# How finely the next tile's projections are dealt out over the first sixteen segments of a recurrent attention block

## The chip, the cores and the metric

The kernel runs on one core of a Trainium2 chip. The metric is the device time of one launch in microseconds (us). The matmul engine is called PE (its weight loads are shown apart, as PEld), the vector engine DVE, the scalar engine ACT, GpSimd POOL; the queue from which most DMAs are issued is that of SP.

## The reference, cut to what matters

Two mixers alternate, A, B, A, B, each with a layer norm before it and a residual behind it. A is the recurrent one, and the change is in it:

```python
for s in range(64):                       # segments of 32 rows, one after the other
    h = concat([mem, xs[s]])              # 8 memory rows + 32 rows of the sequence
    q, k, v = h @ Wq, h @ Wk, h @ Wv      # 32 heads of 128
    p = softmax(mask(q @ k.T * scale))
    o = (p @ v) @ Wo
    mem = o[:8]                           # the next segment starts from these rows
    outs.append(o[8:])
```

B is a gated MLP that mixes over the sequence; the change does not touch it. All is bf16 with float32 sums; the sequence has 2048 rows.

## The kernel before, in words

`a_block` runs twice (below: the first and the second block), each time over 64 segments. Four segments make a tile of 128 rows, so a block has 16 tiles; `tb` is the tile and `j4` the segment in it, 0 to 3.

A segment needs the last memory rows of the segment before it, so the segments are a chain. The last 8 rows of the 32 of each segment of the sequence are kept apart ("old" rows): their projections do not depend on the memory and are made ahead, for all four segments of the next tile at once. That is `b_units` (L753). It makes six chunks, named by `j`: 0 and 1 are the two halves of the queries, 2 and 3 of the keys, 4 and 5 of the values. A chunk is 16 matmuls of 512 columns (four steps of the contraction, `kt`, times four column groups that run side by side). It is summed in one bank of PSUM, either that of the pool `accA` or that of `accB`. Both pools have one buffer. In every segment `accB` serves, one after the other, the query half 1 (`psm`), the value half 1 (`psV`), the output products `px` and the chunk of old rows.

The order of PE, DVE and ACT is the order in which the program is written (`manual_schedule`). POOL and SP are ordered by the scheduler. `b_units` is a generator; `segment` (L908) calls it through `fill()`, three times a segment, at places where PE would else wait:

- fill 1, ahead of `pv(0)`: after the scores and their sums, while ACT and DVE still make the second half of the weights `E` (L960, L963);
- fill 2, after `pv(1)`: while the memory rows are normalised (`memory_out`, L1021) that `wo_pairs` (L794) needs;
- fill 3, after the output products `px` (`wo_pairs`, L794) and `pw` (`wo_rest`, L801): while DVE folds `px` (`fold`, L891 and L893), adds it to `pw` (L898) and turns the sum into the next segment's input `hT` (L900). The next segment begins with the matmuls `psQ` on that input.

Two chunks are spent per segment, one in each pool. Of the `accA` chunk four matmuls go to fill 1, eight to fill 2 and four to fill 3; the whole `accB` chunk goes to fill 3, behind them. So fill 3 has 20 matmuls. In the first 16 segments of a block a tile's six chunks are done in segments 0, 1 and 2 (order 4, 5, 0, 2, 1, 3), and segment 3 has none. From tile 4 on, segment 3 carries parts of the output product of the old rows (`y_part`). In tile 0 of the first block the next tile's chunks are made before, in segment 0.

What a chunk leaves behind is copied out of PSUM by ACT when `run(copies)` comes: after the memory rows (ahead of `wo_pairs`), and after fill 3. Value chunks go to `VB`; when both are there, `store_v` (L737) writes them to DRAM in one DMA of 256 KB, and `spread_v` (L740), called from `tail` in segment 1, reads them back in four DMAs of 64 KB as `VX`. Query and key chunks go to `rowsB` (two slots), and one DMA transpose each (L780, issued from SP) writes them to `QTB` and `KTB`.

`prep_segment` (L877) picks a segment's part from `QTB` and `KTB` on POOL: one copy to `QQ` and two to `KX` (L885), for the two halves `r` of the heads. `scores(0)` needs half 0 of `KX`, `scores(1)` half 1. In the kernel before both halves lie in one tile `KX`, of which there are two for even and odd segments. POOL also copies `hB` (L637), the old rows of the next tile's input, once per tile; it waits for the DMA transpose of `hT` (L208).

Of the kernel before, what the change touches and what calls it, by code (L numbers as in the profile page):

```python
# [7 lines left out]
BF16 = mybir.dt.bfloat16  # L8
F32 = mybir.dt.float32
# [5 lines left out]
P = 128  # L15
DM = 512
KT = 4
# [564 lines left out]
def qk_rhs(w, j, kt, cg):  # L582
    return w[j // 2][:, kt, :].rearrange("p (r gs i eb el) -> p r eb i gs el", r=2, gs=4, i=4, eb=4)[:, j % 2, cg]


def cols_rhs(w, j, kt, cg):
    at = 2048 * (j % 2) + 512 * cg
    return w[j // 2][:, kt, at:at + 512]
# [81 lines left out]
def a_block(tc, c, rows, front, MV_in, RS_in, MV_out, RS_out, ahead, wo, S, first):  # L670
    nc = tc.nc
    NSEG = S // SEG
    NB = S // P
# [3 lines left out]
    with ExitStack() as ctx:  # L677
# [12 lines left out]
        pers = ctx.enter_context(tc.tile_pool(name="a_pers", bufs=1))  # L690
# [7 lines left out]
        accA = _Tagged(acc_pool, "accA", 1)  # L698
        accB = _Tagged(acc_pool, "accB", 1)
# [7 lines left out]
        w = ahead.wqkv  # L707
# [4 lines left out]
        def mm_chunk(ps, lhs, rhs, kts=range(KT)):  # L712

            return [nc.tensor.matmul(ps[32 * cg:32 * cg + 32, :], lhsT=lhs(kt, cg), rhs=rhs(kt, cg), start=(kt == 0), stop=(kt == KT - 1),  # L714
                                     tile_position=(0, 32 * cg)) for kt in kts for cg in range(4)]
# [8 lines left out]
        NKQ = 2  # L724
        KAr = [pers.tile([P, 2, 8, 32, 2], BF16, name=f"KA{i}") for i in range(2)]
        QQr = [pers.tile([P, 2, 8, 40, 2], BF16, name=f"QQ{i}") for i in range(NKQ)]
        KXr = [pers.tile([P, 4, 2, 32], BF16, name=f"KX{i}") for i in range(NKQ)]
        uT = [pers.tile([P, H, 32], BF16, name=f"uT{i}") for i in range(2)]
        for t in uT:
            (nc.vector if first else nc.gpsimd).memset(t[:], 0.0)  # L730
# [1 line left out]
        blk_state = {}  # L732
# [4 lines left out]
        def store_v(bs):  # L737
            nc.sync.dma_start(rows.vb_d[:], bs["VB"].rearrange("p i r e -> p (i r e)"))
# [7 lines left out]
        rowsB = rowp.tile([P, 2, 512], BF16, name="rowsB", bufs=1)  # L746
        copies, turns, adds = [], [], []

        def run(todo):
            while todo:  # L750
                todo.pop(0)()

        def b_units(tb, early=0, alone=False):  # L753
            bs = blk_state[tb]
            order = (0, 2, 1, 3, 4, 5) if early else (4, 5, 0, 2, 1, 3)

            for k, j in enumerate(order):
                now = k < early
                ps = (accB if k % 2 and not alone and not (now and j == 5) else accA).tile([P, 512], F32, name="psb")[:]
                for kts in (((0,), (1, 2), (3,)), ((0, 1, 2, 3),))[k % 2 or alone]:  # L760
                    mm_chunk(ps, lambda kt, cg: bs["hB"][:, kt, :],
                             lambda kt, cg: qk_rhs(w, j, kt, cg) if j < 4 and now else cols_rhs(w, j, kt, cg), kts)
                    if kts[-1] != KT - 1:
                        yield

                def out(k=k, j=j, ps=ps, now=now):
                    if j >= 4:
                        nc.scalar.copy(bs["VB"][:, :, j - 4, :], ps.rearrange("p (i e) -> p i e", i=4))
                        if now:
                            ahead.regroup(bs["VB"], bs["VX"], (j - 4,))  # L770
                        elif j == (5 if alone else 4):
                            store_v(bs)
                        return
                    r = rowsB[:, k % 2, :]
                    nc.scalar.copy(r, ps)
                    t = bs[("QTB", "KTB")[j // 2]][:, j % 2]
                    if now:
                        turns.append(lambda: nc.vector.transpose(out=t.rearrange("p a b -> p (a b)"), in_=r))
                    else:
                        nc.sync.dma_start_transpose(out=t.rearrange("p (i g) k -> p i (g k)", g=4), in_=r.rearrange("t (i e) -> t i e", i=4))  # L780

                if now or k % 2 == 0:
                    copies.append(out)
                else:
                    copies.insert(0, out)
                if now or k % 2 or alone:
                    yield

        def wo_pairs(px, lhs):
# [81 lines left out]
        def y_norm(tb, store):  # L871
            rows.y_norm(tb, MV_out[:, tb, 0:1], RS_out[:, tb:tb + 1], store)
# [4 lines left out]
        def prep_segment(s, eng=nc.gpsimd):  # L877
            tb, j4 = s // 4, s % 4
            bs = blk_state[tb]
            QQ = QQr[s % NKQ]  # L880
            eng.tensor_copy(QQ[:].rearrange("p r n q two -> p (r n) two q")[:, :, :, 32:40],
                            bs["QTB"].rearrange("p r (n two) k -> p (r n) two k", two=2)[:, :, :, 8 * j4:8 * j4 + 8])
            KX = KXr[s % NKQ]
            for r in range(2):
                eng.tensor_copy(KX[:, :, r].rearrange("p g (k i) -> p i g k", i=4),  # L885
                                      bs["KTB"][:, r].rearrange("p (i g) k -> p i g k", i=4)[:, :, :, 8 * j4:8 * j4 + 8])
            seg_state[s] = dict(QQ=QQ, KX=KX, VX=bs["VX"])

# [19 lines left out]
        def segment(s, fill, spare1, spare2, spare3, tail, loads):  # L908
            tb, j4 = s // 4, s % 4
            st = seg_state.pop(s)  # L910
            QQ, KX, VX = st["QQ"], st["KX"], st["VX"]
# [10 lines left out]
            def qk(j, ps, copy=nc.scalar.copy):  # L922
                mms = mm_chunk(ps, lambda kt, cg: hA_cur[:, kt, :], lambda kt, cg: qk_rhs(w, j, kt, cg))
                r = rowp.tile([P, 512], BF16, name="rows", tag="rowsQK", bufs=3)
                return r, mms, copy(r[:].rearrange("p (n el two) -> p n el two", n=8, two=2), ps.rearrange("p (n two el) -> p n el two", n=8, two=2))  # L925
# [7 lines left out]
            def ends(q):  # L933

                return q.rearrange("p h (b e) -> p h b e", e=8)[:, :, 0:5:4, :]

            def own(q):

                return q.rearrange("p (i b e) -> p i b e", i=4, b=2)
# [4 lines left out]
            def scores(r):  # L944

                pS = psS[:, r, :]
                mms = []
                for i in range(4):
                    for g in range(4):
                        n = 4 * i + g  # L950
                        mms.append(nc.tensor.matmul(pS[32 * g:32 * g + 32, 40 * i:40 * i + 40], lhsT=KA[:, r, n // 2, :, n % 2], rhs=QQ[:, r, n // 2, :, n % 2],  # L951
                                                    start=(i == 0), stop=True, tile_position=(0, 32 * g), skip_group_check=True))
                for g in range(4):
                    q = QQ[:, r].rearrange("p (i g) q two -> p i g two q", i=4)[:, :, g // 2, g % 2, :]
                    mms.append(nc.tensor.matmul(own(pS[32 * g:32 * g + 32, 160:224]), lhsT=KX[:, g, r, :], rhs=ends(q),  # L955
                                                start=False, stop=True, tile_position=(0, 32 * g), skip_group_check=True))
                return mms

# [73 lines left out]
            r2, mms, _ = qk(2, psQ[:, 1, :])  # L1032
# [86 lines left out]
            if s + 1 < NSEG:  # L1119
                prep_segment(s + 1)  # L1120
# [28 lines left out]
        def values(units):  # L1149
            for n in (3, 1):  # L1150
                for _ in range(n):
                    next(units)
                run(copies)
                yield

        for s in range(NSEG):
            tb, j4 = s // 4, s % 4
            if first and s == 0:
                more = values(units)
            elif j4 > 0 and tb == NB - 1:  # L1160
                more = y_part(tb // 4, j4 - 1, last=True)
            elif j4 == (3 if tb < NB - 1 else 0) and tb > 3:
                more = y_part(tb // 4 - 1, tb % 4)
            elif first and s == 1:
                more = iter(())
            elif j4 == (first and tb == 0):
                more = b_units(tb + 1)
            if j4 == (tb == 0) and tb + 2 < NB:
                rows.load(tb + 2, first, nc.sync)

# [47 lines left out]
                        y_stats(NB - 6, k)  # L1218

            def tail():  # L1220
                if j4 == 1 + 2 * (first and tb == 0) and tb + 1 < NB:
                    spread_v(blk_state[tb + 1])
                if tb == NB - 1:
                    if j4 != 2:
                        front.load_w(j4)
                    if j4 > 0:
                        front.load_rows(j4 - 1)
                if ys and ys[0][1]:
                    y_norm(ys.pop(0)[0], nc.sync)
                for y in ys:  # L1230
                    y[1] = True
                if j4 == 0 and tb > 7 and (tb % 4 == 0 or tb == NB - 1):
                    due.extend(range(tb // 4 * 4 - 8, tb // 4 * 4 - 4) if tb < NB - 1 else range(NB - 8, NB - 4))
# [20 lines left out]
        ends = (uT[NSEG % 2], oBs[NB // 4 - 1][:, :, 96:128])  # L1254
# [52 lines left out]
```

## Time and profile before

| what | us |
|---|---|
| three runs | 1625.49, 1628.31, 1628.37 (median 1628.31) |
| the profiled execution's own time | 1627.99 |
| its span, first to last instruction | 1626.3 |
| granted PE clock, mean | 0.999 |
| PE busy | 1579.0 (97%) |
| ACT, DVE, POOL busy | 1047.4, 1065.8, 290.4 |

A line of the profile's timeline gives start, duration, engine, line, operation, output and inputs, and the number of instructions merged into it; in brackets the idle time of the engine just before it and what ended that. A matmul's record covers its whole way through the engine, so records of matmuls that follow each other overlap. Below, a segment's length is taken from one start of the exponential of `scores(0)` (the first L960 of a segment) to the next. In the second block these starts are at 919.58, 929.61, 939.65, 949.68 and 959.32 us for the four segments of tile 2 and the first one of tile 3.

### The profile page before, as it was taken

Reading aid. Unit: us, or ns where it says so; the run is one execution under the profiler, and the core shown is the slowest. Engines: PE = TensorE matmul, PEld = TensorE weight load, DVE = VectorE, ACT = ScalarE, POOL = GpSimd, SP = SyncE. Lnnn points to the kernel's source line nnn. Section 1 sums busy time; section 2 is a strip of 40 time slices with the busy share of each in tenths; the row PEclk is TensorE's granted clock in tenths of the full one; section 3 lists DMA queues with packets and bytes.
Section 4 is the critical chain, followed back from the end, with each engine's and each line's share of the span. In section 5 each row is a group of like instructions: output and inputs, shape, how many; then the busy total and the mean of one; then the engine's idle time right before and its main releaser. Section 6 shows DMA issues by size and latency. Waiting matters only on the chain.

```text
span 1626.3 us, 90252 instructions
## 1 busy us (share of the span) xinstructions
PE 1579.0 (97%) x40647; PEld 976.1 (60%) x40670; DVE 1065.8 (66%) x3052; ACT 1047.4 (64%) x2281; POOL 290.4 (18%) x604
## 2 busy tenths in 40 slices
PE   5899999999999999999999999999999999999999
PEld 2556566666666666566656555666666666665565
DVE  4566666667776776784466666666677667767722
ACT  3677777777777777660047777777777777766400
POOL 6111111112211221320011111111121112224000
PEclk9999999999999999999999999999999999999999
DMA  9412111123321343377951222122232223425797
GB/s 362 96 41 47 43 43 43 43 43 82 84 46 43 87 85 77 92 183 162 213 156 46 46 46 46 47 46 47 72 92 71 47 71 96 97 53 171 140 191 169
DMA packets 263611, 148.97 MB, mean 92 GB/s; under 512 B 197561, under 2 KB 239649, under 8 KB 263225
## 3 DMA queue, kind: packets, MB, share of 16 engines
q1 hardware_dynamic: 249992, 99.38, 28.2%
q0 software_dynamic: 13232, 43.82, 8.3%
q8 instruction: 318, 5.21, 1.3%
q14 instruction: 69, 0.56, 0.1%
HBM read 59.68 MB, written 37.19 MB: 60 GB/s over the span
## 4 chain that ended last, share of the span: by engine, by line
PE 53%; DVE 2%; DMA 1%; issue 1%; POOL 1%; ACT 0%; POOLq 0%; SPq 0%
PE pg L397 9%; PE psQ L714 7%; PE psK L714 7%; PE psb L714 5%; PE px L794 4%; PE psm L714 3%; PE psV L714 3%; PE psO L801 3%; PE pz L296 3%; PE py L440 2%; PE pwB L813 1%; PE psO L1000 1%; PE psT L992 1%; PE psS L951 1%; PE psS L974 0%
## 5 line engine op out<-in xcount | busy, mean ns | idle before, releaser
L714 PEld LDWEIGHTS <-hT 128*32 128x32 bf16 x12288 | 338.5, 97 | 274.1 <-DVE hT L900 13.3
L928 DVE STREAM_TRANSPOSE QQ<-rows 128x256 f32<-128x256 f32 x256 | 113.3, 443 | 80.9 <-ACT rows L925 79.8
L714 PE MATMUL psV<-Wv_sb,hT 128*32 128x512 bf16 x2048 | 165.6, 379 | 0.0
L1024 DVE TENSOR_TENSOR uT<-psO,Rt 128x384 bf16<-128x384 f32 x256 | 140.2, 548 | 29.2 <-ACT Rt L1100 28.8
L925 ACT CAST rows<-psQ 128x512 bf16<-128x512 f32 x256 | 142.8, 594 | 23.3 <-PE psQ L714 22.7
L960 ACT ACTIVATE S<-psS 128x224 bf16<-128x224 f32 x256 | 92.2, 360 | 97.5 <-PE psS L955 97.3
L1021 DVE TENSOR_TENSOR uT<-psO,Rm 128x128 bf16<-128x128 f32 x256 | 74.6, 291 | 122.6 <-ACT Rm L1018 120.6
L397 PE MATMUL pg<-z,wspT 128*128 128x344 bf16 x1024 | 154.3, 309 | 0.0
L714 PE MATMUL psK<-Wv_sb,hT 128*32 128x512 bf16 x2048 | 152.7, 378 | 0.0
L1100 ACT ACTIVATE Rt<-Rt 128x512 f32<-128x512 f32 x256 | 147.2, 622 | 4.1
L928 DVE STREAM_TRANSPOSE KA<-rows 128x256 f32<-128x256 f32 x256 | 112.9, 441 | 53.5 <-ACT rows L925 46.5
L714 PE MATMUL psQ<-Wq_sb,hT 128*32 128x512 bf16 x2048 | 135.8, 381 | 11.6 <-DVE hT L900 6.8
L794 PEld LDWEIGHTS <-uT 128*32 128x32 bf16 x4608 | 122.4, 97 | 34.4 <-DVE uT L1021 3.6
L794 PE MATMUL px<-Wo,uT 128*32 128x256 bf16 x3840 | 133.7, 273 | 2.1 <-issue 0.8
L714 PE MATMUL psQ<-Wk_sb,hT 128*32 128x512 bf16 x2048 | 135.5, 381 | 0.0
L714 PE MATMUL psK<-Wk_sb,hT 128*32 128x512 bf16 x2048 | 134.8, 379 | 0.0
L714 PE MATMUL psm<-Wq_sb,hT 128*32 128x512 bf16 x2048 | 134.8, 379 | 0.0
L885 POOL COPY KX<-old 128x128 bf16<-128x128 bf16 x128 | 68.3, 534 | 364.0 <-PE psS L955 225.7
L1097 ACT ACTIVATE Rt<-psT 128x1024 f32<-128x1024 f32 x128 | 131.1, 1024 | 3.1
L397 PEld LDWEIGHTS <-wspT 128*128 128x128 bf16 x1024 | 100.2, 98 | 53.2
L801 PE MATMUL psO<-Wo_high,uT 128*32 128x128 bf16 x7168 | 125.8, 219 | 4.1 <-issue 3.5
L885 POOL COPY KX<-front 128x128 bf16<-128x128 bf16 x126 | 65.2, 524 | 347.5 <-PE psS L955 202.0
(200 smaller groups left out, 2913.8 us busy)
## 6 DMA issues: line engine op xcount, KB each, us to landing
o_d<-o_sb SPq DMA_DIRECT2D x126, 64.0 KB
vb_d<-front SPq DMA_DIRECT2D x30, 256.0 KB
VX<-vb_d SPq DMA_DIRECT2D x120, 64.0 KB
ln_x<-xd SPq DMA_DIRECT2D x26, 256.0 KB
y_o<-o_d POOLq DMA_DIRECT2D x22, 256.0 KB, 3.2
xd<-y_o POOLq DMA_DIRECT2D x22, 256.0 KB, 3.0
Wq_sb<-in_A_Wq_dram POOLq DMA_DIRECT2D x8, 512.0 KB, 9.3
Wk_sb<-in_A_Wk_dram POOLq DMA_DIRECT2D x8, 512.0 KB, 10.0
```

The lines of the kernel that those rows point to most:

```text
L397: nc.tensor.matmul(pg[t][:, k, 0:344], lhsT=wsp[t][:, st, :], rhs=z(st, 344 * k, 344 * k + 344), start=(st == 0), stop=(st == NT - 1))
L714: return [nc.tensor.matmul(ps[32 * cg:32 * cg + 32, :], lhsT=lhs(kt, cg), rhs=rhs(kt, cg), start=(kt == 0), stop=(kt == KT - 1), tile_posi ...
L794: nc.tensor.matmul(px[at:at + 32, 0:256], lhsT=lhs[:, h, :], rhs=wo_rhs(h, slice(k + 2, None, -2) if h % 2 else slice(k, None, 2)), start= ...
L801: nc.tensor.matmul(pw[32 * cg:32 * cg + 32, :], lhsT=lhs[:, h, :], rhs=wo_rhs(h, cg), start=False, stop=(h == H - 1), tile_position=(0, 32 ...
L885: eng.tensor_copy(KX[:, :, r].rearrange("p g (k i) -> p i g k", i=4), bs["KTB"][:, r].rearrange("p (i g) k -> p i g k", i=4)[:, :, :, 8 * ...
L925: return r, mms, copy(r[:].rearrange("p (n el two) -> p n el two", n=8, two=2), ps.rearrange("p (n two el) -> p n el two", n=8, two=2))
L928: nc.vector.transpose(out=(QQ[:, j % 2, :, 0:32] if j < 2 else KA[:, j % 2]).bitcast(F32).rearrange("p n q one -> p n (q one)"), in_=r[:]. ...
L960: return nc.scalar.activation(out=S[:, r], in_=psS[:, r, 0:224], func=ACT.Exp, scale=scale)
L1021: nc.vector.tensor_tensor(out=hview(uT_cur[:], r, 24, 32), in0=oview(r, 0, 8), in1=Rm[:, r].rearrange("p g (n q) -> p g n q", q=8), op=ALU ...
L1024: nc.vector.tensor_tensor(out=hview(uT_nxt[:], r, 0, 24), in0=oview(r, 8, 32), in1=rview(r, 0, 24), op=ALU.mult)
L1097: nc.scalar.activation(out=Rt[:], in_=psT[:], func=ACT.Ln)
L1100: nc.scalar.activation(out=rt, in_=rt, func=ACT.Exp, scale=-1.0)
```

## The change

For tiles 0 to 3 of a block (where the next tile's chunks are not made otherwise) `b_even` takes the place of `b_units`. It spends one and a half chunks in each of the four segments: nothing in fill 1, eight matmuls of an `accA` chunk in fill 2, and one whole `accB` chunk (16 matmuls) in fill 3. Chunk 4 is spread over segments 0 and 1 beside 5 and 0; chunk 2 over segments 2 and 3 beside 1 and 3. The copies of chunks 4 and 2 thus fall ahead of `wo_pairs` in segments 1 and 3, those of the others behind fill 3. `store_v` moves from the end of segment 0 to the middle of segment 1, `spread_v` from segment 1 to segment 2. The last key chunk, 3, is finished at the very end of segment 3. In all segments of both blocks `KX` becomes two tiles, one for each half `r`.

This concerns tiles 1, 2, 3 of the first block and 0, 1, 2, 3 of the second: seven tiles, 28 segments.

```diff
-        KXr = [pers.tile([P, 4, 2, 32], BF16, name=f"KX{i}") for i in range(NKQ)]
+        KXr = [[pers.tile([P, 4, 32], BF16, name=f"KX{i}{r}") for r in range(2)] for i in range(NKQ)]
...
+        def b_out(bs, slot, j, ps, turned, stored):
...
+        def b_mms(bs, j, ps, kts, turned=False):
+            mm_chunk(ps, lambda kt, cg: bs["hB"][:, kt, :],
+                     lambda kt, cg: qk_rhs(w, j, kt, cg) if j < 4 and turned else cols_rhs(w, j, kt, cg), kts)
...
+        def b_even(tb):
+
+            bs = blk_state[tb]
+            for j, others in ((4, (5, 0)), (2, (1, 3))):
+                psA = accA.tile([P, 512], F32, name="psb")[:]
+                for kts, other in zip(((0, 1), (2, 3)), others):
+                    yield
+                    b_mms(bs, j, psA, kts)
+                    if kts[-1] == KT - 1:
+                        copies.append(lambda j=j, psA=psA: b_out(bs, 0, j, psA, False, True))
+                    yield
+                    psB = accB.tile([P, 512], F32, name="psb")[:]
+                    b_mms(bs, other, psB, range(KT))
+                    copies.append(lambda other=other, psB=psB: b_out(bs, 1, other, psB, False, False))
+                    yield
...
-                eng.tensor_copy(KX[:, :, r].rearrange("p g (k i) -> p i g k", i=4),
+                eng.tensor_copy(KX[r][:].rearrange("p g (k i) -> p i g k", i=4),
...
-                    mms.append(nc.tensor.matmul(own(pS[32 * g:32 * g + 32, 160:224]), lhsT=KX[:, g, r, :], rhs=ends(q),
+                    mms.append(nc.tensor.matmul(own(pS[32 * g:32 * g + 32, 160:224]), lhsT=KX[r][:, g, :], rhs=ends(q),
...
-                more = b_units(tb + 1)
+                more = (b_even if tb < 4 else b_units)(tb + 1)
...
-                if j4 == 1 + 2 * (first and tb == 0) and tb + 1 < NB:
+                if j4 == (3 if first and tb == 0 else 2 if tb < 4 else 1) and tb + 1 < NB:
                     spread_v(blk_state[tb + 1])
```

`b_out` holds, word for word, what the function `out` inside `b_units` did. The order of POOL changes where one tile goes over into the next: before, the three copies of one segment stand together; after, POOL's order there is `QQ`, `QQ`, `hB`, `KX` half 0 of segment 0, half 0 of segment 1, half 1 of segment 0, half 1 of segment 1. On SP the transposes stand one by one instead of in pairs, and in segment 3 the order is the transpose of `hT` (L208), the load of the rows (L196), the transpose of chunk 2, the store of the output (L906), the transpose of chunk 3.

More of the change, by code (lines that the diff above doesn't have):

```diff
@@ L751, in run @@
                 todo.pop(0)()
+        def b_out(bs, slot, j, ps, turned, stored):
+            if j >= 4:
+                nc.scalar.copy(bs["VB"][:, :, j - 4, :], ps.rearrange("p (i e) -> p i e", i=4))
+                if turned:
+                    ahead.regroup(bs["VB"], bs["VX"], (j - 4,))
+                elif stored:
+                    store_v(bs)
+                return
+            r = rowsB[:, slot, :]
+            nc.scalar.copy(r, ps)
+            t = bs[("QTB", "KTB")[j // 2]][:, j % 2]
+            if turned:
+                turns.append(lambda: nc.vector.transpose(out=t.rearrange("p a b -> p (a b)"), in_=r))
+            else:
+                nc.sync.dma_start_transpose(out=t.rearrange("p (i g) k -> p i (g k)", g=4), in_=r.rearrange("t (i e) -> t i e", i=4))
+        def b_mms(bs, j, ps, kts, turned=False):
+            mm_chunk(ps, lambda kt, cg: bs["hB"][:, kt, :],
+                     lambda kt, cg: qk_rhs(w, j, kt, cg) if j < 4 and turned else cols_rhs(w, j, kt, cg), kts)
         def b_units(tb, early=0, alone=False):
@@ L760, in b_units @@
                 for kts in (((0,), (1, 2), (3,)), ((0, 1, 2, 3),))[k % 2 or alone]:
-                    mm_chunk(ps, lambda kt, cg: bs["hB"][:, kt, :],
-                             lambda kt, cg: qk_rhs(w, j, kt, cg) if j < 4 and now else cols_rhs(w, j, kt, cg), kts)
+                    b_mms(bs, j, ps, kts, now)
                     if kts[-1] != KT - 1:
@@ L766, in out @@
                 def out(k=k, j=j, ps=ps, now=now):
[L767 to L780, printed above, removed]
+                    b_out(bs, k % 2, j, ps, now, j == (5 if alone else 4))
                 if now or k % 2 == 0:
```

## The prediction

> **What bounds the kernel now.** First the page: how busy each engine is.
>
> ```profile
> span 1626.3 us, 90252 instructions
> PE 1579.0 (97%) x40647; PEld 976.1 (60%) x40670; DVE 1065.8 (66%) x3052; ACT 1047.4 (64%) x2281; POOL 290.4 (18%) x604
> ```
>
> PE is the bound by a wide margin, so what the change is worth lies in PE's idle time inside the 28 segments it touches. Next, the sums by stretch for the four segments of tile 2 in the second block and the first of tile 3 (columns: stretch and length, then busy time of each engine).
>
> ```profile
> 919.58:929.61 10.03, 10.03 (x312) 6.16 (x304) 6.46 (x19) 7.69 (x18) 1.50 (x4) 1.00 0.12 37
> 929.61:939.65 10.04, 10.04 (x312) 6.15 (x304) 6.46 (x19) 7.70 (x19) 1.51 (x4) 1.00 0.23 55
> 939.65:949.67 10.02, 10.02 (x312) 6.16 (x304) 6.46 (x19) 7.68 (x18) 0.67 (x2) 1.00 0.17 36
> 949.67:959.32 9.65, 8.75 (x280) 5.28 (x272) 6.96 (x20) 6.93 (x16) 2.33 (x6) 1.00 0.37 59
> ```
>
> A segment with two chunks (32 matmuls) takes 10.03 us and PE shows no hole; the one with none takes 9.65 with 0.90 of hole. The first three differ from the last by 32 matmuls but by 0.38 us only. If a matmul cost just its issue time, sharing out evenly would gain. So the third view is where the holes of the empty segment lie (the timeline, its three waits):
>
> ```profile
> 951.18 0.39 DVE L963 TENSOR_TENSOR E<-S,maskN 128x448 bf16<-128x448 bf16 x1
> 951.63 0.45 PE L992 MATMUL psT<-E,ones 64*128 64x512 bf16 x4
> ...
> 953.74 0.26 ACT L1095 COPY cross<-px 64x128 f32<-64x128 f32 x1 [0.72 <-PE px L794]
> ...
> 955.15 0.61 PE L714 MATMUL psQ<-Wq_sb,hT 128*32 128x512 bf16 x8 [0.68 <-DVE hT L900]
> ```
>
> and the fourth is the end of a full segment, around fill 3:
>
> ```profile
> 923.82 0.28 DVE L891 COPY cross<-px 64x128 f32<-64x128 f32 x1 [0.60 <-PE px L794]
> 924.21 0.29 DVE L893 TENSOR_TENSOR t<-px,cross 128x128 f32<-128x128 f32 x1
> 924.37 1.25 PE L714 MATMUL psb<-Wv_sb,hB 128*32 128x512 bf16 x20
> 924.60 0.29 DVE L898 TENSOR_TENSOR memT<-psO,t 128x128 bf16<-128x128 f32 x1
> 924.99 0.37 DVE L900 STREAM_TRANSPOSE hT<-memT 128x64 bf16<-128x64 bf16 x2
> 925.45 0.60 PE L714 MATMUL psQ<-Wq_sb,hT 128*32 128x512 bf16 x8
> ```
>
> The 20 matmuls start in five rounds of four, at 924.37 and 925.45 for the next work: (925.45 - 924.37) / 5 = 0.216 us a round. `accB` is still held by `px` until L893 has read it, at 924.21 + 0.29 = 924.50. PE starts 0.06 after a DVE result (951.18 + 0.39 = 951.57, `psT` at 951.63), so a matmul into `accB` can start at 924.56. Today the first round goes to `accA` and the second, into `accB`, starts at 924.59: the wait is there, just hidden.
>
> **The change part by part.**
>
> *Fill 1 loses four matmuls: 0.* `psT` starts 0.06 after `E` in both kinds of segment: 951.63 - 949.68 = 1.95 us into the empty one, and 921.53 - 919.58 = 1.95 into a full one. The hole takes the round for nothing, so taking it out gives nothing back.
>
> *Fill 2 keeps its eight: 0.* In segment 3 they are new, and with fill 3 they make it a segment like the others.
>
> *Fill 3 goes from 20 to 16: -0.03.* Its first round now goes to `accB`, so it starts at 924.56, not 924.37, and its four rounds end at 924.56 + 4 x 0.216 = 925.42, against 925.45. The input `hT` is no limit there: in the empty segment `psQ` follows the start of L900 (954.85) by 0.30, which puts it at 925.29 in the full one. So a segment with 1.5 chunks takes 10.00 us. Bounds: 9.87 if the `px` wait were nothing (fill 3 would end at 925.23, and `hT` at 925.29 decide), 10.03 if nothing is gained.
>
> *Segment 3: +0.35* (9.65 to 10.00).
>
> Sum of a tile of the second block: -3 x 0.03 + 0.35 = +0.26, for four tiles +1.04.
>
> *First block.* Its segments measure 10.03, 10.03, 10.11 and 9.66. At the end of segment 1 two small ACT operations of the row statistics stand in the list of copies ahead of the chunk. Before, the `accB` copy was put in front of them; now it is appended behind, so `psm`, which needs `accB`, comes later. Ln and Exp take 0.30 + 0.20, about 0.45 in line; the copy ends 7.64 us into the segment, and `psm` would start 5.84 + 1.73 = 7.57: late by 0.13 with the 0.06. Tile: 4 x 10.00 + 0.13 - 39.83 = +0.30, for three tiles +0.9.
>
> *Moved at no cost.* The copies of chunks 4 and 2 by ACT (0.56 each) fall ahead of `cross`, where ACT has the 0.72 of idle time shown; if that were gone, `cross` and with it L893 would be late by the rest. The one copy less behind fill 3 lets the `rows` casts begin earlier, but PE is not waiting for them: from `psQ` to the scores takes 4.17 in both kinds of segment. `store_v` and the four `spread_v` DMAs come a segment later and have one segment left; SP's waits for them hold back only output stores and transposes that nobody needs within 5 us. The split of `KX` changes no instruction.
>
> *The tile's seam: +2.1.* Chunk 3 now ends with segment 3, and `scores(1)` of the very next segment needs what comes of it: ACT copy, SP issue, DMA transpose, POOL copy of `KX` half 1. Before, the same chain had a whole empty segment. Its rows (SP, then POOL; normal, then late; last the `hB` copy that POOL now has ahead of `KX`):
>
> ```profile
> 946.90 2.50 SPq L780 DMA_TRANSPOSE old<-rowsB  x2
> 949.46 0.48 POOL L885 COPY KX<-old 128x128 bf16<-128x128 bf16 x1 [9.35 <-DMA old<-rowsB]
> 986.64 3.56 SPq L780 DMA_TRANSPOSE front<-rowsB  x2
> 990.85 0.46 POOL L885 COPY KX<-front 128x128 bf16<-128x128 bf16 x1 [11.01 <-PE psS L974]
> 957.26 0.29 POOL L637 COPY hB<-hT 128x128 bf16<-128x128 bf16 x1 [3.23 <-DMA hT<-ln_xn]
> ```
>
> The issue comes 946.90 - 939.65 = 7.25 us into the segment, `scores(1)` loads `KX` at 5.84 + 4.97 = 10.81. Less 0.48 for the copy and 0.06, issue to copy may take 3.02. It takes 2.56 normally and 4.21 in the late row; at 27 tile ends that I can pair, eight lie above 3.02, late by 0.19 to 1.20, in the mean over all 0.19. New beside it: the transpose of chunk 2 stands on SP behind that of `hT` and the row load (1.19 + 0.57, up to 1.87 for the load alone), and POOL's `KX` half 0 stands behind it and behind `hB`, which lands up to 2.3 us into the segment; `scores(0)` needs it at 3.76. I add 0.11, an estimate from these rows. 7 x 0.30 = 2.1; ends 0 and 7 x 1.20 = 8.4.
>
> Here a rule speaks against the change. A `KX` copy takes 0.48 alone and up to 0.70 beside DVE's work. The Trainium skill, SBUF — State Buffer, "Who interferes with whom", says that a DVE instruction with two SBUF inputs and a GpSimd instruction that reads SBUF exclude each other. By it a late `KX` copy would also wait for the first `E` (0.35): 7 x 8/27 x 0.35 = 0.7 more, 1632.7 in place of my time. The trace agrees as far as it goes: the copy of 0.70 at 952.65 lies beside a DVE operation of 952.34 that took 0.68, where the same one took 0.54 at 912.52.
>
> Sum: 1.04 + 0.9 + 2.1 = +4.0, against the profiled execution's own 1627.99: **1632.0 us**. That execution lies 0.3 below the median 1628.31. About 0.2% (3.3 us) is what a measurement of this kernel can tell from no change; slower begins at 1631.6.
>
> **Rivals.** *The seam is in time.* The mean chain has 0.46 to spare (3.02 - 2.56). For it: 19 of 27 rows. Against: seven tiles, each with three transposes and a load near the seam. 1627.99 + 1.9 = 1629.9, no measurable change. *The seam is always late*, the three transposes queueing up: 7 x 1.0 (the mean of the upper four late rows) = 7.0, 1627.99 + 1.9 + 7.0 = 1636.9. *The `px` wait is no wait* (not slower): if L893 came 0.19 us earlier against PE, fill 3 would start at 924.37 and the segment take 9.87. A second-block tile would be 39.48 for 39.74, a first-block one 39.61 for 39.83: 4 x -0.26 + 3 x -0.22 = -1.7, with the seam in time 1626.3. It decides from an L893 that ends at 924.31; all full segments show it at 924.50 against the same PE rows, so I give it little. Only with scatter on top would it count as faster. *The change does nothing* to the order is out: the built program has it, with the wait on DVE ahead of fill 3's first matmul.
>
> **How the numbers follow.** Forecast (seam late now and then) 0.58; in time 0.24; always late 0.12; fill 3 without its wait 0.06. Of the forecast's cases about 7 in 10 lie above 1631.6. Slower 0.58 x 0.7 + 0.12 + 0.02 of the second = 0.55; same 0.39; faster 0.06, from the last case and unseen ones. Range 1628.5 to 1637.0: the second case less 1.4 of scatter (the three runs spread 2.9), the third with a little over.
>
> **What would show it.** Right: segments of 10.00 in all four places, 0.2 of PE idle time ahead of fill 3 released by L893, `psT` still 1.95 in. At the seam some waits of PE for POOL's `KX`, up to a microsecond, and none elsewhere. Wrong: segments at 9.7 to 9.85, or seams with no wait at all, or with one in each tile.

## The result, and the profile after

The changed kernel took 1634.62 us (median of six runs, 1633.75 to 1638.72); the kernel before took 1628.34 beside it (six runs, 1625.49 to 1629.61). The ratio is 1.0048, with a 95% interval of 1.0033 to 1.0062. A ratio here is worked out from all runs and not from the two medians: by it the change is about 7.8 us slower, by the medians 6.3. The profiled execution's own time was 1633.75 us.

The page first, as for the kernel before:

```profile
span 1632.0 us, 90242 instructions
PE 1589.4 (97%) x40670; PEld 982.4 (60%) x40670; DVE 1067.9 (65%) x3052; ACT 1049.9 (64%) x2281; POOL 288.6 (18%) x604
```

PE's share stands at 97% as before, in a kernel that is slower with the same matmuls. The share says nothing about this change.

Now the sums by stretch, each from one start of the exponential of `scores(0)` to the next. The first stretch is segment 3 of tile 1 of the second block, then come the four segments of tile 2 and the first two of tile 3 (columns: stretch and length, then busy time and instructions of PE, PEld, DVE, ACT, POOL, then granted clock, DMA share and GB/s).

```profile
914.42:924.42 10.00, 9.93 (x304) 6.34 (x296) 6.92 (x20) 7.82 (x19) 1.82 (x5) 1.00 0.36 76
924.42:934.84 10.42, 10.13 (x304) 6.39 (x296) 6.47 (x19) 7.35 (x18) 2.05 (x6) 1.00 0.05 12
934.84:944.83 9.99, 9.92 (x304) 6.35 (x296) 6.46 (x19) 7.83 (x18) 1.49 (x3) 1.00 0.18 54
944.83:954.83 10.00, 9.94 (x304) 6.37 (x296) 6.47 (x19) 7.32 (x18) 0.20 (x1) 1.00 0.19 45
954.83:964.82 9.99, 9.93 (x304) 6.33 (x296) 6.92 (x20) 7.80 (x18) 1.83 (x5) 1.00 0.39 77
964.82:976.58 11.76, 10.13 (x304) 6.40 (x296) 6.58 (x19) 7.36 (x18) 1.98 (x6) 1.00 0.03 9
976.58:986.58 10.00, 9.93 (x304) 6.42 (x296) 6.47 (x19) 7.84 (x19) 1.49 (x3) 1.00 0.22 63
```

All stretches hold the same 304 matmuls. Five of the seven take 10.00, whichever place they have in the tile. The two that don't, 10.42 and 11.76, are the first segments of a tile.

The end of an undisturbed segment (that of 934.84), from the timeline:

```profile
939.07 0.28 DVE L914 COPY cross<-px 64x128 f32<-64x128 f32 x1 [0.59 <-PE px L817]
939.46 0.29 DVE L916 TENSOR_TENSOR t<-px,cross 128x128 f32<-128x128 f32 x1
939.80 1.05 PE L714 MATMUL psb<-Wq_sb,hB 128*32 128x512 bf16 x16
939.85 0.29 DVE L921 TENSOR_TENSOR memT<-psO,t 128x128 bf16<-128x128 f32 x1
940.18 0.37 DVE L923 STREAM_TRANSPOSE hT<-memT 128x64 bf16<-128x64 bf16 x2
940.66 0.61 PE L714 MATMUL psQ<-Wq_sb,hT 128*32 128x512 bf16 x7
```

(From here on the changed file's lines are meant: those behind the new functions lie 23 further down, so `t` of L893 is L916 and the `KX` copy of L885 is L908.) The fold ends at 939.46 + 0.29 = 939.75; fill 3 starts 0.05 later and `psQ` 0.86 after that. Fill 3 now has 16 matmuls, waits for `px` in the open, and the segment ends 0.03 earlier than the full one of before. The wait hardly shows as idle time of PE, since the record of the last matmul of `pw` reaches to 939.80. It shows in the starts: that matmul starts at 939.58, so the first of fill 3 comes 0.22 behind it, where in the kernel before it came 0.05 behind (924.33 and 924.37).

The long segment of 964.82 begins with the seam from tile 2 to tile 3. SP's queue, then POOL, then PE's weight loads, in three answers of the timeline:

```profile
958.09 1.19 SPq L208 DMA_TRANSPOSE hT<-ln_xn  x1
959.33 0.57 SPq L196 DMA_DIRECT2D ln_x<-xd  x1
960.00 1.97 SPq L768 DMA_TRANSPOSE old<-rowsB  x1
962.07 0.55 SPq L929 DMA_DIRECT2D o_d<-o_sb  x1
962.73 1.20 SPq L768 DMA_TRANSPOSE old<-rowsB  x1
```

```profile
963.77 0.77 POOL L908 COPY KX<-old 128x128 bf16<-128x128 bf16 x2 [2.91 <-DMA old<-rowsB]
966.88 1.06 POOL L908 COPY KX<-old 128x128 bf16<-128x128 bf16 x3 [2.34 <-DMA old<-rowsB]
```

```profile
967.40 0.10 PEld L978 LDWEIGHTS <-KX 128*32 128x32 bf16 x4 [1.70 <-POOL KX L908]
```

SP works from 958.09 to 963.93 with gaps of no more than 0.11. The transpose of chunk 3 is the fifth in line and is issued 962.73 - 954.83 = 7.90 us into segment 3; its data lets POOL begin half 1 of `KX` only at 966.88, and PE loads it at 967.40, 12.57 into the stretch that began at 954.83. An undisturbed seam loads it at 10.80. That is 1.77 us in one place.

Who waits for `KX`, over the whole span (the view of one tile; after each name: microseconds, times), first in the kernel after, then in that before:

```profile
who waited for it (us, times):
  POOL KX L908: 367.3, 70
...
  PEld L978: 5.0, 8
  PE psS L978: 4.1, 7
```

```profile
who waited for it (us, times):
  POOL KX L885: 427.8, 81
  ACT S L960: 97.3, 127
  POOL QQ L881: 43.7, 62
  POOL front L174: 0.6, 2
```

PE's weight loads wait for `KX` eight times in the kernel after, and never before. (The row counts idle time alone; where a load is late, the loads behind it shift too.) Taken against the normal places of the two loads (9.59 us into segment 3 for half 0, half 1 1.21 later; in the last seam 0.26 is left out, by which its segment 3 is longer without a wait for `KX`), the seven seams lose 0.87, 0.36, 0.14 (first block) and 1.05, 0.44, 1.77, 1.14 (second): 5.8 us. Half 0 has 1.55 of it, in three seams; half 1 has 4.2.

The account: the seven tiles and the tile behind each block's last seam take 7.1 us longer than before (2.05 in the first block, 5.02 in the second). The forecast's terms for the segments, 1.94, and the 5.8 of the seams make 7.7; a segment of 10.68 in the second block that is 10.35 now gives back 0.3 of that. That is 7.4, or 0.3 more than measured. The two spans differ by 5.7 only, for stretches that the change does not touch moved as well: +0.6 us ahead of these tiles, +1.5 between the two blocks, -3.4 behind the last of them. So the loss is read from the tiles, and not from the spans.

### The profile page after: what moved, and what is told of

Read it like the earlier page. It is cut to its first block, busy times and chain, and to the rows that moved or that the text cites. A ratio compares the mean times of both kernels' runs of the same rounds, so it can differ in the third digit from the quotient of the medians.

```text
span 1632.0 us, 90242 instructions
## 1 busy us (share of the span) xinstructions
PE 1589.4 (97%) x40670; PEld 982.4 (60%) x40670; DVE 1067.9 (65%) x3052; ACT 1049.9 (64%) x2281; POOL 288.6 (18%) x604
## 3 DMA queue, kind: packets, MB, share of 16 engines
q8 instruction: 318, 5.21, 1.3%
## 4 chain that ended last, share of the span: by engine, by line
PE 53%; DVE 1%; DMA 1%; ACT 1%; issue 1%; POOL 0%; DVEq 0%; POOLq 0%; SPq 0%
PE pg L397 9%; PE psQ L714 6%; PE psK L714 6%; PE psb L714 5%; PE pz L296 5%; PE px L817 4%; PE psm L714 3%; PE psV L714 3%; PE psO L824 3%; PE py L440 2%; PE pwB L836 2%; PE psO L1023 1%; PE psT L1015 1%; PE psS L974 1%; PE pw L1282 0%
## 5 line engine op out<-in xcount | busy, mean ns | idle before, releaser
L817 PEld LDWEIGHTS <-uT 128*32 128x32 bf16 x4608 | 123.2, 97 | 32.4 <-issue 2.3
L908 POOL COPY KX<-old 128x128 bf16<-128x128 bf16 x128 | 65.9, 531 | 311.0 <-PE psS L978 191.0
L824 PEld LDWEIGHTS <-uT 128*32 128x32 bf16 x7168 | 114.2, 97 | 2.7 <-issue 1.5
```

The costliest lines, as they stand in the source:

```text
L817: nc.tensor.matmul(px[at:at + 32, 0:256], lhsT=lhs[:, h, :], rhs=wo_rhs(h, slice(k + 2, None, -2) if h % 2 else slice(k, None, 2)), start= ...
L824: nc.tensor.matmul(pw[32 * cg:32 * cg + 32, :], lhsT=lhs[:, h, :], rhs=wo_rhs(h, cg), start=False, stop=(h == H - 1), tile_position=(0, 32 ...
```

## The experiments

The theory: with its segments at 10.00 the change costs 1.9, and the rest is the seam, where the keys come too late by way of SP's queue. The rivals: the rest is something else that the change moved (the split of `KX`, the values' store, ACT's copies); PE is bound by its matmuls, and an even share would gain if the rounds were placed rightly; the 1634.62 was chance. Ratios are to the kernel before, whose median was 1626.0 in the one set of runs (the keys by DVE, the keys first, the split, the rounds 1, 1, 4) and 1625.9 in the other.

### The changed kernel again

> The kernel after once more, on the chip of this call, as a measure for the run with the rows loaded by ACT. Theory: ratio 1.004 to 1.005, segments of 10.00, five to seven of fourteen seam places late, 4 to 6 us of waits. Rival (the first profile of the kernel after caught an unusual execution): waits of 2 us or less, as forecast.

1632.41 us, ratio 1.0043 (1.0031 to 1.0056). Another profile of the same program lost 1.06, 0.76 and 0 at the seams of the first block, where the first one lost 0.87, 0.36 and 0.14, and 1.26, 0.55, 0.17 and 0.95 at those of the second; the sum is 4.75 us. The account closes here too: 1.94 and 4.75 less 0.3 are 6.4, and the same tiles take 6.6 longer than in the kernel before. Its rows of who waited for `KX`:

```profile
  PEld L978: 3.9, 7
  PE psS L978: 3.0, 5
```

The waits at the seam are there again, in other sizes from seam to seam. The change is slower by 0.4 to 0.5%, and not by chance.

### The keys turned by DVE in place of the DMA

```diff
 def b_even(tb):
+    def out(slot, j, ps):
+        if j not in (2, 3):
+            return b_out(bs, slot, j, ps, False, j == 4)
+        r = rowsB[:, slot, :]
+        nc.scalar.copy(r, ps)
+        t = bs["KTB"][:, j % 2]
+        adds.append(lambda: nc.vector.transpose(out=t.rearrange("p a b -> p (a b)"), in_=r))
+    def mms(j, ps, kts):
+        b_mms(bs, j, ps, kts, j in (2, 3))
...
-                    b_mms(bs, j, psA, kts)
+                    mms(j, psA, kts)
...
```

> The kernel after, but the two key chunks of b_even are turned by DVE at the end of their segment instead of by a DMA transpose, so KX does not wait for SP at the tile's seam. Theory (segments of 10.00 us each, +1.9 us in all, and the rest of the loss is the late KX at seven seams): segments of 10.00, no wait for KX, 1630.2 us, ratio 1.0012. Rival (the loss lies in the evenly spent segments themselves, the seam is only where it shows): ratio stays at 1.004 to 1.005. Second rival (only the seam costs): ratio 1.000 or below.

1628.95 us, ratio 1.0015 (1.0006 to 1.0024), or by the ratio 2.4 us over the kernel before. Segments take 9.99 to 10.00, the first one behind a seam 10.08 (the turn on DVE costs it 0.08), and PE waits for no `KX`. So without the chain over SP and POOL at the seam about 2 us are left, which is what the segments cost; two thirds of the loss are the seam.

### The keys first

```diff
-            for j, others in ((4, (5, 0)), (2, (1, 3))):
+            for j, others in ((2, (3, 0)), (4, (1, 5))):
...
-                        copies.append(lambda j=j, psA=psA: b_out(bs, 0, j, psA, False, True))
+                        copies.append(lambda j=j, psA=psA: b_out(bs, 0, j, psA, False, False))
...
-                    copies.append(lambda other=other, psB=psB: b_out(bs, 1, other, psB, False, False))
+                    copies.append(lambda other=other, psB=psB: b_out(bs, 1, other, psB, False, other == 5))
```

The same work in the same share, every DMA transpose kept, but the keys are done in segments 0 and 1 and the values last; the values come too late for their tile, which uses older ones.

> The kernel after with the chunks in the order 2, 3, 0, 4, 1, 5, so keys and queries are ready a segment before the seam; all DMA transposes stay. The value chunks come too late for their round trip through DRAM, so the old rows' values of the tile before are used: the output is not the reference's. Theory: no wait for KX at the seam, segments of 10.00, ratio 1.0012 like the turn by DVE. Rival (it is the single DMA transposes spread over the tile, not their lateness): ratio stays at 1.004 or above.

1626.37 us, ratio 1.0003 (0.9991 to 1.0014). The last two segments of tile 2 of the second block and the first of tile 3:

```profile
942.03:952.03 10.00, 9.93 (x304) 6.36 (x296) 6.46 (x19) 7.32 (x18) 1.17 (x3) 1.00 0.11 23
952.03:962.02 9.99, 9.92 (x304) 6.35 (x296) 6.92 (x20) 7.80 (x18) 1.95 (x5) 1.00 0.25 77
962.02:972.02 10.00, 10.00 (x304) 6.46 (x296) 6.58 (x19) 7.32 (x18) 1.51 (x4) 1.00 0.22 51
```

No seam waits for `KX`, and the seam's part of the loss is gone. So it is not the transposes as such, but that the last of them starts at the very end of the tile. The expected 1.9 us lie inside the interval; this run alone would also allow 0.

### The row load issued by ACT

```diff
-                rows.load(tb + 2, first, nc.sync)
+                rows.load(tb + 2, first, nc.scalar if tb < 5 else nc.sync)
```

> The kernel after with the load of the rows (L196) issued by ACT a segment later, in tiles 0 to 4, so SP has one DMA less between the transpose of hT and those of chunks 2 and 3. Theory (the seam is late because SP still works off that queue when the copy of chunk 3 is ready, 7.25 us into segment 3): the transpose of chunk 3 is issued 0.4 to 0.6 us earlier, the waits for KX fall from 6 us over seven seams to about 2, ratio 1.002 to 1.003. Rival (the transposes land late whatever SP does): the waits stay, ratio 1.005.

1629.86 us, ratio 1.0025 (1.0013 to 1.0036). SP's queue at the seam from tile 2 to tile 3 of the second block (segment 3 begins at 954.23):

```profile
957.49 1.19 SPq L208 DMA_TRANSPOSE hT<-ln_xn  x1
958.77 2.00 SPq L768 DMA_TRANSPOSE old<-rowsB  x1
960.86 0.51 SPq L929 DMA_DIRECT2D o_d<-o_sb  x1
961.49 1.19 SPq L768 DMA_TRANSPOSE old<-rowsB  x1
```

(The load stays in segment 3; ACT issues it 6.1 us into the segment, where SP did at 4.5.) One DMA of some 0.6 us less on SP ahead of the transpose of chunk 3, and that is issued 7.26 us into the segment, though chunk 2's transpose again took 2.00. Over the seven seams the issue comes at 7.31 in the mean, against 7.87 in both profiles of the changed kernel, and 1.55 us of waits remain of 5.8 and 4.75:

```profile
  PEld L978: 1.3, 3
  PE psS L978: 1.0, 3
```

In this set of runs the changed kernel stood at 1.0043, so the move saves some 2.9 us, about what the waits lost. SP's queue is the larger part of the seam's loss, with one limit: the load's own traffic moved by 1.6 us too, and no run parts the two.

### The split of KX alone

```diff
-        KXr = [pers.tile([P, 4, 2, 32], BF16, name=f"KX{i}") for i in range(NKQ)]
+        KXr = [[pers.tile([P, 4, 32], BF16, name=f"KX{i}{r}") for r in range(2)] for i in range(NKQ)]
```

with the two places that use it, and nothing else of the change.

> The kernel before with only KX split into two tiles, one for each half. Theory: no segment changes, ratio 1.000 within 0.001. Rival (the split tiles or POOL's other order cost time in all 128 segments): a part of the 1.005.

1626.94 us, ratio 1.0004 (0.9995 to 1.0013), segments of 10.03 and 9.65 as before. No gain or cost is seen; the interval alone would allow up to 2 us.

### The kernel before without fill 1

```diff
                 for kts in (((0,), (1, 2), (3,)), ((0, 1, 2, 3),))[k % 2 or alone]:
-                    mm_chunk(...)
+                    short = not (k % 2 or alone or now)
+                    if not short or kts != (0,):
+                        mm_chunk(..., kts, int(short))
```

The first quarter of the contraction is left out in the chunks that go to `accA`, in all tiles but those made ahead. These are the chunks 4, 0 and 1, and not 4, 0 and 2 as the expectation has it. The profile counts 40670 weight loads of PE in the kernel before and 40322 here, so 348 matmuls are gone (the expectation has 360): 87 rounds of 0.216, or 18.8 us by PE's issue time.

> The kernel before with fill 1 left out in every tile: the first quarter of the contraction of the chunks 4, 0 and 2 is not computed (360 matmuls, 90 rounds of 0.216 us, 19.4 us of PE time less), so the output is not the reference's. Theory (fill 1 lies in a hole until E is there): segments stay at 10.03, ratio 1.000. Rival (PE is the bound by its count): segments of 9.81, 19 us less, ratio 0.988.

1627.04 us, ratio 1.0007 (0.9995 to 1.0019). The first segment of tile 2 of the second block:

```profile
918.34:928.37 10.03, 10.03 (x308) 6.21 (x300) 6.47 (x19) 7.70 (x19) 1.49 (x4) 1.00 0.11 37
```

308 matmuls take the same 10.03 as 312 did. A round in fill 1 is free; to take it away, as the change does, gives nothing back.

### Rounds 0, 1, 5: fill 3 begins with the other bank

```diff
+                    mms(j, psA, kts[:1])
                     yield
-                    b_mms(bs, j, psA, kts)
+                    mms(j, psA, kts[1:])
+                    if kts[-1] == KT - 1:
+                        copies.append(lambda j=j, psA=psA: out(0, j, psA))
                     psB = accB.tile([P, 512], F32, name="psb")[:]
...
+                    copies.insert(0, lambda other=other, psB=psB: out(1, other, psB))
```

Keys turned by DVE as above, and one of the two `accA` rounds of fill 2 put at the front of fill 3 (20 matmuls again). All copies now fall behind fill 3, and that of `accB` goes to the front of their list, as in the kernel before.

> Keys turned by DVE, rounds 0, 1, 5: four matmuls into accA stand ahead of the accB chunk in fill 3, instead of in fill 1. Theory (an accA round in fill 3 costs nothing because accB is not free before L893 has read px): measured from the 9.80 of rounds 1, 1, 4 the wait of 0.18 is filled by a round of 0.216, so segments of 9.83 to 9.84, ratio 0.997. Rival (there is no such wait, a round more in fill 3 costs its 0.216): segments of 10.02, ratio 1.001.

1624.16 us, ratio 0.9990 (0.9979 to 1.0000). The first two segments of tile 2 of the second block, and the end of the second one:

```profile
919.88:929.71 9.83, 9.83 (x304) 6.07 (x296) 6.47 (x19) 7.31 (x18) 1.56 (x4) 1.00 0.04 12
929.71:939.54 9.83, 9.76 (x304) 5.91 (x296) 6.47 (x19) 7.70 (x18) 1.55 (x3) 1.00 0.12 23
```

```profile
934.13 0.29 DVE L929 TENSOR_TENSOR t<-px,cross 128x128 f32<-128x128 f32 x1
934.30 0.39 PE L714 MATMUL psb<-Wv_sb,hB 128*32 128x512 bf16 x4
934.52 1.03 PE L714 MATMUL psb<-Wq_sb,hB 128*32 128x512 bf16 x16
```

The fold (L929 here) ends at 934.42. The round into `accA` starts at 934.30, before that, and the first into `accB` at 934.52 with no hole between. The same 24 matmuls take 9.83 for 10.00. That gain of 0.17 is two things at once: a round less in fill 2, and a round more in fill 3. The next section parts them: the rounds 1, 1, 4 also leave one round in fill 2, have four in fill 3 and take 9.80. Against them the fifth round of fill 3, 0.216 long, makes the segment 0.03 longer, so about 0.19 of it lies in the wait for `px`.

### Rounds 1, 1, 4

```diff
+                    mms(j, psA, kts[:1])
                     yield
-                    b_mms(bs, j, psA, kts)
+                    mms(j, psA, kts[1:])
```

Keys turned by DVE; one `accA` round in fill 1, one in fill 2, the `accB` chunk in fill 3.

> Keys turned by DVE as in the run before, and four of fill 2's eight matmuls moved back to fill 1: rounds 1, 1, 4 in place of 0, 2, 4. Same number of matmuls. Theory (fill 1 has a hole for one round, fill 2 for one round less than two, fill 3 waits for L893): everything from px on comes 0.16 us earlier, segments of 9.84, a tile 39.36 against 39.77 before, in all -2.7 us, 1625.6, ratio 0.9983. Rival (PE is the bound and only the number of matmuls counts): segments of 10.00 as in the turn by DVE, ratio 1.0012.

1621.8 us, ratio 0.9966 (0.9954 to 0.9979): by the ratio 5.5 us faster than the kernel before, by the medians 4.2, and the fastest of all here. The first two segments of tile 2 of the second block, then the end of the second one:

```profile
917.44:927.32 9.88, 9.88 (x304) 6.15 (x300) 6.46 (x19) 7.31 (x17) 1.64 (x4) 1.00 0.04 12
927.32:937.12 9.80, 9.80 (x304) 6.15 (x296) 6.46 (x19) 7.79 (x19) 1.50 (x3) 1.00 0.19 55
```

```profile
931.74 0.29 DVE L929 TENSOR_TENSOR t<-px,cross 128x128 f32<-128x128 f32 x1
932.09 1.05 PE L714 MATMUL psb<-Wq_sb,hB 128*32 128x512 bf16 x16
932.95 0.62 PE L714 MATMUL psQ<-Wq_sb,hT 128*32 128x512 bf16 x8
```

The fold ends 932.03 - 927.32 = 4.71 us into the segment, where it was 4.91 in the changed kernel, and all behind it is earlier by as much. So the second round of fill 2 had cost 0.20 a segment: moved into the free hole of fill 1, it costs nothing. The tiles take 39.3 to 39.7 us, against 39.7 to 40.5 before.

## Why the prediction was right, and where its sum was not

The direction was right, and the time is inside the range; the forecast of 1632.0 was 2.6 us low. There is luck in that: the range reached up to 1637.0 because it took in the rival "always late", and that rival's seam is nearer to the measured one than the forecast's.

- *What bounds the kernel.* That a matmul's price depends on the hole it falls into was right. That PE is the bound by a wide margin, read from its 97%, was not: without fill 1, 18.8 us of matmuls go from PE and nothing is gained; one round moved from fill 2 to fill 1 saves 0.20 in a segment.
- *Fill 1: 0.* Shown by leaving it out.
- *Fill 2 keeps its eight: 0.* Right for this change, since the eight stay. But the sentence passed over what they cost where they are, which the rounds 1, 1, 4 show to be 0.20 for the second round.
- *Fill 3: -0.03, by the `px` wait.* The forecast had `psQ` 5.84 us into the segment and the segment at 10.00; it came at 940.66 - 934.84 = 5.82, and at 10.00. The wait itself is shown by the rounds 0, 1, 5, which fill it, and by the starts at 939.58 and 939.80; as 0.2 of idle time, which the forecast expected to see, it does not show. The rival of 9.87 is out for the order as it was changed.
- *Segment 3: +0.35.* 10.00, as said.
- *First block.* Forecast for its second segments 10.13, with the row statistics ahead of the `accB` copy; they measure 10.11 to 10.12.
- *Moved at no cost.* Segments of 9.99 to 10.00 leave no room for another cost of ACT's copies or the values' store; the split of `KX` alone measures 1.0004.
- *The tile's seam: +2.1.* This is the step that failed, in size: it measured 5.8 in one profile and 4.75 in the other, nearer to the 7.0 of the rival "always late" than to 2.1. All seven seams were late in the one, six in the other: what the forecast itself had named as a sign that it would be wrong. The place and the chain were right (the keys, not the values; the runs with the keys first and with the keys by DVE have no such wait). The term that was mis-sized is the issue of chunk 3's transpose. The step took it at 7.25 us, the place it had at the end of another segment, and covered SP's queue with 0.11. It came at 7.87 in the mean of the seven (7.28 to 8.13), since SP had a transpose of `hT`, a row load, chunk 2's transpose and an output store to issue first, one after the other. The step's own figures, with that place in them, come much nearer: it put the issue-to-copy time at 2.56 normally, with 8 of 27 later than 3.02, by 0.64 in the mean. With 0.62 more, the 19 normal ones are late by 2.56 + 0.62 - 3.02 = 0.16 and the other eight by 1.26, 0.49 in the mean, or 3.4 us for seven. With the row load moved away the issue came at 7.31 and the waits were 1.55; for an issue at 7.25 the step's figures give 7 x 0.19 = 1.3. Of what 3.4 leaves of the 5.8, half 0 has the larger part, late in three seams by 1.55 together: chunk 2's transpose is in that queue too, and the step gave it no price of its own.
- *The rule weighed against the trace.* The Trainium skill, SBUF — State Buffer, "Who interferes with whom", lets a GpSimd copy wait out a DVE instruction with two SBUF inputs. The trace agrees, but the price is smaller than the prediction's 0.35. Two copies of `KX`, each with the `E` that it began beside, from the kernel before and from the one after:

```profile
275.77 0.35 DVE L963 TENSOR_TENSOR E<-S,maskN 128x448 bf16<-128x448 bf16 x1
275.85 0.61 POOL L885 COPY KX<-front 128x128 bf16<-128x128 bf16 x1 [10.16 <-PE psK L714]
```

```profile
442.58 0.39 DVE L986 TENSOR_TENSOR E<-S,maskN 128x448 bf16<-128x448 bf16 x1
442.58 0.72 POOL L908 COPY KX<-front 128x128 bf16<-128x128 bf16 x1 [2.83 <-PE psS L997]
```

The first copy began 0.08 behind its `E`, the second with it; they end 0.34 and 0.33 behind the end of `E`. In the ten profiles 667 copies began within 0.2 us of the start of an `E`. Each ended 0.32 to 0.35 behind it, whenever it had begun, and took 0.52 to 0.72 in place of 0.48. So about 0.15 of a copy lies ahead of the wait, and `E` costs it at most 0.24. At the seven seams of the changed kernel the copy of half 1 that PE waits for took 0.47 to 0.55; this is not where the 5.8 come from.

What stays open: the first segment of the second block's tile 1 takes 10.35 to 10.41 in five of the ten profiles (10.68 in the kernel before, 10.03 with the split of `KX` alone), and segment 3 of its tile 3 takes 10.25 or 10.26 in four, without a wait for `KX`. These were counted to neither side.

## What to carry to other kernels

Filler dealt out evenly is no gain in itself. Each hole has a size, and where the first round of a hole must wait for its bank of PSUM, that wait costs nothing only if a round for another bank stands before it. Moving work to the end of a period moves its whole chain of DMAs to the seam, so add up, from the rows of the trace, every DMA that the queue must issue ahead of it, the ones with nothing to do with the change included. Here one round per hole and the keys turned without a DMA made of a loss of 0.5% a gain of 0.3%.

## What the runs showed of the hardware that was not expected

- A DMA transpose of one chunk occupies SP for 1.19 to 1.24 us, or for 1.5 to 2.6. Of the 930 such transposes in eight of these profiles (all but the keys by DVE and the rounds 1, 1, 4), 686 took no more than 1.24, 176 took over 1.5, and 68 lie between. The data lands mostly 1.0 to 1.3 us behind the issue's end (544 of the 901 whose sixteen parts are all there within 4 us), or 2.2 and more (253).
- Which of them it is goes with the packets of 16 KB on the queues that the profile calls "instruction" (318 packets with 5.21 MB on the larger one in the kernel after, about 1.1 us each). In 143 of the 176 long issues such a packet began between 0.3 us before and 0.9 us after the issue's start; of the 754 others that holds for 35. In 98 of the 901 the last part came over 0.5 us behind the one before it, and in 87 of these a packet had begun between the issue's end and the landing; in the other 803, in 124.
- In the seam shown above one of these packets began 0.74 us after the end of chunk 3's issue and took 1.08; 15 of the 16 parts of the transpose were there by 965.30, the last at 966.83. At the seam from tile 3 to tile 4 of the second block such a packet began at the very end of the issue in both profiles of the changed kernel, and all parts were late (2.3 to 2.7). That is a coincidence in time in many cases; no run took the packets away, so it isn't shown as a cause. It would explain why the same seams vary from one execution to the next.
- PE at 97% busy left room for 18.8 us of matmuls to be taken out without effect.
